# Output weights of a fused attention and token-mixing kernel: one load and cast per block, with the swapped arrangement copied on chip

## The chip, the cores and the metric

The kernel runs on one core of one Trainium2 chip. The metric is the device time of one execution in microseconds (us), the median of several runs. The engines of the core are named as in the profile: PE is TensorE (PEld its weight loads), DVE is VectorE, ACT is ScalarE, POOL is GpSimd, SP is SyncE, which here only issues transfers. Each engine works through its own instructions in order; what one engine makes and another reads is guarded by a semaphore.

## What is computed

A sigmoid attention, whose output, with the heads laid side by side, is the input of a token mixer with an output projection:

```python
# q, k, v: (8, 12, 448, 64)
scores = scale * np.matmul(q, k.transpose(0, 1, 3, 2)) - np.log(S)
attn = 1.0 / (1.0 + np.exp(-scores))
x = np.matmul(attn, v)                       # then transposed to (8, 448, 768)
wq = x @ w_q                                 # (8, 448, 64)
wk = x @ w_k
W_tok = (1.0 / np.sqrt(64)) * np.einsum('bsd,btd->bst', wq, wk)
mixed = np.einsum('bst,btd->bsd', W_tok, x)
out = np.maximum(mixed, 0.0) @ w_out         # w_out: (768, 768)
```

Inputs and output are float32; the kernel computes its matmuls in bf16.

## The kernel before

The 12 heads of each of the 8 batch entries are taken four at a time: 24 quads (a "quad" is one batch entry u and one group j of four heads). For each quad the kernel loads q, k and v (448 KB each, line 180), casts them to bf16 on GpSimd (L199), transposes q and k on TensorE (L221 for whole 128 x 128 blocks, L213 for 64 x 64 blocks) and evacuates them from PSUM to a `qk` tile on VectorE (L246 or L251). Seven score steps S(n, 0..6) of quad n follow (`scores`, L263: four matmuls, then one sigmoid on ScalarE, L268, of 128 x 896 elements), and seven value steps P(n, 0..6) (`values`, L281), which accumulate in PSUM; after the seventh VectorE evacuates the result to `xt` (L290).

When the three quads of a batch entry are done, the mixer's steps run: W (`mlp_wqk`, L345, evacuated by VectorE at L350; GpSimd then copies half of it to the other partitions at L354), x (transposes back to tokens, L304 or L321, evacuated at L309 or L334), N, U, M (the mixing, with the relu at L387) and O, the output projection. The projection is done in two ways. Batch entries 0, 1, 6 and 7 go through `out_chunk` (L481), whose matmuls contract over 128 partitions and read slots 0 to 5 of the weight tile. Entries 2 to 5 go through `out_pair` (L446), whose matmuls contract over 64 partitions, the two halves of the partitions working side by side; half y of the partitions needs block b of 64 weight rows, and as both halves need all twelve blocks, the weight tile holds each block twice, once in either half. `slot(half, b)` says where.

The weight tile `wout16` is 128 partitions x 12 slots x 768, in bf16. Slots 0 to 5 hold rows 128c to 128c + 127 of `w_out`. Slots 6 to 11 hold the same rows shifted by 64, so that each block also stands in the other half. Each slot is one load of 384 KB (`load_wout`, L527 to L535; the last slot takes two loads of 192 KB) and one cast on GpSimd (L603).

Nothing is left to a scheduler. The order of the work is written out: `PLAN` is a string with one letter for each step (S, P, W, x, N, U, M, O, and q/k transposes as a/b or q/k), worked through from left to right, and every step emits its instructions on all engines that it uses at that point. `ORDER` is the order of the loads and casts; `w0` is the pair of mixer weights, `w1` to `w12` the slots of `wout16`. Two pumps run along with the plan. `pump_loads` issues the next load on SP as long as the fifth load before it has had its cast emitted (`ld` has five buffers). `pump` emits the next cast on GpSimd as soon as its load has been issued and, for q and k, the cast two before it has been transposed, for v, the cast three before it has been used up. `pump` is called after each transposing step and after the last value step of a quad, so a cast may be emitted long before its data have landed: it then waits on GpSimd.

PSUM is one tile of eight banks, used as four pairs. `bank2` hands out the pair at the front of the list `free2`, and `release` puts it at its end at the point where the evacuation is emitted. A step that is handed a pair waits for the evacuation of what was in it.

The step that the prediction speaks of first is S(3,1), the second score step of quad 3, the row of L263 at 27.35 us; the pair that it is handed is the one in which the q and k of quad 5 were transposed. P(5,0), at 47.29 us, is handed the pair of quad 9. The lines that order the loads and casts of the weights are

```python
if nm == "w":
    if n:
        nc.gpsimd.tensor_copy(out=wout16[:, n - 1, :], in_=w32[n - 1])
```

Of the kernel before, what the change touches and what calls it, by code (L numbers as in the profile page):

```python
# [16 lines left out]
def kernel(  # L17
# [14 lines left out]
    nc = tc.nc  # L32
# [4 lines left out]
    P = 128  # L37
# [3 lines left out]
    NC = D // P  # L41
    NB = D // 2
    HALF = (slice(0, 64), slice(64, 128))
# [50 lines left out]
    wout16 = singles.tile([P, 2 * NC, D], BF16, name="wout16")  # L94
# [93 lines left out]
    def cast1(n, nm, eng):  # L188
        if twice(nm, n):
            t16 = p_c16.tile([P, 2, NI, 32, 2], BF16, tag=nm + "16", name=nm + "16")  # L190
            eng.tensor_copy(
                out=t16.rearrange("p h i d y -> p h y i d"),
                in_=ld.pop((nm, n)).rearrange("p h (y i d) -> p h y i d", y=2, d=HD)[..., 0:32],
            )
            ld[nm + "16", n] = t16
            return
        p = p_v16 if nm == "v" else p_c16
        t16 = p.tile([P, NI, 2, HD], BF16, tag=nm + "16", name=nm + "16")
        eng.tensor_copy(  # L199
            out=t16.rearrange("p i b d -> p b i d"),  # L200
            in_=ld.pop((nm, n)).rearrange("p b (i d) -> p b i d", i=NI),
        )
        ld[nm + "16", n] = t16
# [223 lines left out]

    def slot(half, b):

        if b % 2 == half:  # L430
            return b // 2
        return 6 + (b - 1) // 2 if b else 11

    def out_pair(act):

# [7 lines left out]
        for b in range(3 * part, 3 * part + 3):  # L443
            for y, (u, i) in enumerate(blocks):
                for x in range(2):
                    nc.tensor.matmul(  # L446
                        ps[HALF[x], y, 0:NB], mx[HALF[y], u, b, 64 * (i - 3 * y) : 64 * (i - 3 * y) + 64],
                        wout16[HALF[y], slot(y, b), x * NB : (x + 1) * NB],
                        start=(b == 0), stop=(b == 11),
                    )  # L450
# [66 lines left out]
    w32 = {}  # L517
# [8 lines left out]

    def load_wout(c):  # L527
        w32[c] = p_ld.tile([P, 2 * NI * HD], F32, tag="ld", name="w32")[:, 0:D]
        if c < NC:
            nc.sync.dma_start(out=w32[c], in_=moe_w_out[c * P : (c + 1) * P, :])  # L530
        elif c < 11:
            nc.sync.dma_start(out=w32[c], in_=moe_w_out[(c - 6) * P + 64 : (c - 5) * P + 64, :])
        else:
            nc.sync.dma_start(out=w32[c][HALF[0]], in_=moe_w_out[704:768, :])
            nc.sync.dma_start(out=w32[c][HALF[1]], in_=moe_w_out[0:64, :])  # L535

    IA, IB = slice(0, 4), slice(4, 7)
    KA, KB = slice(0, 3), slice(3, 7)
# [6 lines left out]
    def cols(r):  # L545
        return slice(r.start * HD, r.stop * HD)
# [9 lines left out]
        out=ident, in_=ident, compare_op=ALU.not_equal, fill=1.0, base=0,  # L556
# [8 lines left out]
    for t in wqks:  # L565
# [3 lines left out]
    ORDER = (  # L569
        "q1 k1 v0 q2 k2 k3 q3 k4 q4 v1 q5 k5 v2 w0 k6 q6 "  # L570
        "v3 q7 w1 w2 q8 k7 v4 v5 k8 q9 k9 q10 k10 w3 q11 w4 "
        "v6 w5 w6 k11 q12 k12 w7 v7 v8 q13 k13 k14 q14 q15 v9 q16 "
        "v10 k15 k16 w8 q17 q18 w9 w10 v11 k17 v12 v13 v14 q19 k18 w11 "
        "q20 w12 v15 k19 k20 k21 v16 q21 v17 k22 v18 v19 v20 q22 q23 k23 "
        "v21 v22 v23 "
    )
    ORDER = [(t[0], int(t[1:])) for t in ORDER.split()]
# [4 lines left out]
    def pump_loads():  # L582
        while len(loaded) < len(ORDER):
            nm, n = ORDER[len(loaded)]
            r, back = (ring2, 1) if twice(nm, n) else (ring, 5)
            mine = [z for z in r if z[0] == nm] if r is ring2 else r
            if len(mine) >= back and mine[-back] not in cast:
                break
            r.append((nm, n))
            if nm == "w":  # L590
                load_wout(n - 1) if n else load_weights()
            else:
                load1(n, nm, nc.sync)
            loaded.add((nm, n))

    def pump():
        while len(cast) < len(ORDER) + 2:
            nm, n = ORDER[len(cast) - 2]
            if (nm, n) not in loaded:
                break  # L600
            if nm == "w":
                if n:
                    nc.gpsimd.tensor_copy(out=wout16[:, n - 1, :], in_=w32[n - 1])  # L603
                else:
                    for h in range(2):
                        for g in range(2):
                            nc.gpsimd.tensor_copy(
                                out=wqk16[HALF[g], h::2],
                                in_=w32["qk"].rearrange("p (c n) -> p c n", c=NC)[HALF[h], g::2],
                            )  # L610
            else:
                back = 3 if nm == "v" else 2
                if n >= back and (nm, n - back) not in used:
                    break
                cast1(n, nm, nc.gpsimd)
            cast.add((nm, n))
            pump_loads()
# [5 lines left out]
    for t16, t32, r, e in ((q016, q0, IA, "v"), (q016, q0, IB, "s"), (k016, k0, KA, "g"), (k016, k0, KB, "g")):  # L623
        COPY[e](
            out=t16[:, r].rearrange("p i b d -> p b i d"),
            in_=t32[:, :, cols(r)].rearrange("p b (i d) -> p b i d", d=HD),
# [14 lines left out]
    tr_part("k", k016, KA, "v")  # L641
    used |= {("q", 0), ("k", 0)}
    pump()

    done = dict.fromkeys("SPqkKxWNUMO", 0)
# [3 lines left out]
    for t in PLAN:  # L649
# [4 lines left out]
        c = done[kind]  # L654
# [4 lines left out]
        elif t == "P":  # L659
            n, i = divmod(c, NI)  # L660
            values(n, i, tail)
            if i == NI - 1:
                used.add(("v", n))
                pump()
        elif kind in "qk":
            tr(c, kind, t)
            used.add((kind, c))
            pump()
        elif t == "K":
            tr_part("k", k016, KB, "v")  # L670
        elif kind == "x":
            tr_x(c, tail, t == "X")
        elif kind == "W":
            mlp_wqk(*divmod(c, NC), tail)
        elif kind == "N":
            mlp_wkn(c)
        elif kind == "U":
            mlp_tmp(c, t == "u")
        elif kind == "M":
            u, x = divmod(c, NC // 2)  # L680
            mlp_mix(u, x, t == "m", tail)
            if x == NC // 2 - 1:
                if u // 2 in TW:
                    chunks.extend((u // 2, ((u % 2, i), (u % 2, 6 - i))) for i in range(3))
                    if u % 2:
                        chunks.append((u // 2, ((0, 3), (1, 3))))
                else:
                    ms = range(3, NI) if u % 2 else range(3)
                    chunks.extend((u // 2, m, nb) for m in ms for nb in range(2))
        elif kind == "O":  # L690
            if (opened or chunks)[0][0] in TW:
                out_pair(t == "o")
            else:
                out_chunk(t == "o", tail)
# [29 lines left out]
```

## Time and profile before

| | |
|---|---|
| time, median of 3 runs | 204.12 us (203.43 to 205.49) |
| span of the profiled execution | 200.3 us |
| that execution's own time | not given beside the profile |
| granted TensorE clock, mean | 0.998 |
| traffic | HBM read 38.14 MB, written 11.01 MB |

| group | count | busy us | mean ns |
|---|---|---|---|
| L268 sigmoid, ACT | 168 | 157.0 | 1012 |
| L263 scores, PE | 672 | 62.4 | 360 |
| L281 values, PE | 672 | 45.9 | 350 |
| L446 projection by halves, PE | 672 | 36.3 | 323 |
| L199 casts of q, k, v, POOL | 70 | 65.2 | 930 |
| L603 casts of the weights, POOL | 12 | 9.9 | 827 |
| L246 and L251 evacuation of q and k, DVE | 23 | 25.1 | 1090 |

The span runs from the first to the last instruction. Matmuls are pipelined, so the busy time of PE and the mean of one matmul are not its pace. An engine's idle time is put down to what ended it. The twelve weight casts start between 32.6 and 102.5 us. A load of one of their blocks takes 4.8 us (median) from its issue on SP until it has landed.

### The profile page before, as it was taken

Reading aid. Unit: us, or ns where it says so; the run is one execution under the profiler, and the core shown is the slowest. Engines: PE = TensorE matmul, PEld = TensorE weight load, DVE = VectorE, ACT = ScalarE, POOL = GpSimd, SP = SyncE. Lnnn points to the kernel's source line nnn. Section 1 sums busy time; section 2 is a strip of 40 time slices with the busy share of each in tenths; the row PEclk is TensorE's granted clock in tenths of the full one; section 3 lists DMA queues with packets and bytes.
Section 4 is the critical chain, followed back from the end, with each engine's and each line's share of the span. In section 5 each row is a group of like instructions: output and inputs, shape, how many; then the busy total and the mean of one; then the engine's idle time right before and its main releaser. Section 6 shows DMA issues by size and latency. Waiting matters only on the chain.

```text
span 200.3 us, 8999 instructions
## 1 busy us (share of the span) xinstructions
PE 187.9 (94%) x3948; PEld 122.1 (61%) x3950; DVE 125.0 (62%) x165; ACT 170.3 (85%) x194; POOL 82.1 (41%) x101
## 2 busy tenths in 40 slices
PE   8995998898999999999999999999999999999990
PEld 7452564455455655665557667778678869665560
DVE  3234375667755877846786856667787774774520
ACT  4798899798989999999889799999899989975520
POOL 2467777677677647558136320305061110000000
PEclk9999999999999999999999999999999999999999
DMA  5999999999999999899999983388704443332575
GB/s 174 317 351 374 292 361 324 357 358 322 356 352 348 367 389 315 293 320 339 285 318 352 338 301 104 86 242 208 256 17 99 105 109 81 84 79 49 142 211 154
DMA packets 29799, 49.73 MB, mean 248 GB/s; under 512 B 3904, under 2 KB 26560, under 8 KB 29760
## 3 DMA queue, kind: packets, MB, share of 16 engines
q1 hardware_dynamic: 29040, 47.78, 74.2%
q10 hardware_dynamic: 720, 1.38, 1.9%
q8 instruction: 31, 0.51, 1.0%
q14 instruction: 8, 0.07, 0.1%
HBM read 38.14 MB, written 11.01 MB: 245 GB/s over the span
## 4 chain that ended last, share of the span: by engine, by line
PE 61%; DMA 26%; POOL 5%; ACT 2%; issue 1%; SPq 1%; ACTq 1%; DVE 1%; POOLq 0%; DVEq 0%
PE banks L446 14%; PE banks L263 12%; PE banks L281 11%; PE banks L481 8%; DMA k<-in_k_dram 8%; DMA q<-in_q_dram 8%; DMA v<-in_v_dram 6%; DMA out_dram<-o 5%; PE banks L345 4%; POOL q L199 2%; PE banks L376 2%; PE banks L221 2%; PE banks L321 2%; PE banks L213 2%; ACT at L268 2%
## 5 line engine op out<-in xcount | busy, mean ns | idle before, releaser
L268 ACT ACTIVATE at<-banks,bias_t 128x896 bf16<-128x896 f32 x168 | 157.0, 1012 | 11.8 <-PE banks L263 9.5
L263 PE MATMUL banks<-qk 64*64 64x448 bf16 x672 | 62.4, 360 | 1.2 <-ACT at L268 0.5
L281 PE MATMUL banks<-at,v 64*64 64x448 bf16 x672 | 45.9, 350 | 0.5 <-issue 0.5
L263 PEld LDWEIGHTS <-qk 64*64 64x64 bf16 x672 | 24.9, 105 | 21.2 <-issue 13.7
L446 PE MATMUL banks<-wout,mx 64*64 64x384 bf16 x672 | 36.3, 323 | 0.0
L199 POOL CAST v<-v 128x896 bf16<-128x896 f32 x24 | 22.4, 933 | 30.5 <-PE banks L281 21.1
L290 DVE CAST xt<-banks 128x896 bf16<-128x896 f32 x23 | 25.1, 1090 | 12.6 <-PE banks L281 12.6
L481 PE MATMUL banks<-wout,mx 128*128 128x384 bf16 (+1 forms) x174 | 31.1, 321 | 0.0
L199 POOL CAST k<-k 128x896 bf16<-128x896 f32 x23 | 21.4, 932 | 18.2 <-PE banks L213 10.5
L281 PEld LDWEIGHTS <-v 64*64 64x64 bf16 x672 | 23.1, 106 | 6.6 <-issue 0.3
L387 DVE TENSOR_SCALAR mx<-banks 128x1024 bf16<-128x1024 f32 (+2 forms) x22 | 22.7, 1044 | 6.9 <-PE banks L411 3.5
L199 POOL CAST q<-q 128x896 bf16<-128x896 f32 x23 | 21.4, 932 | 9.3 <-DMA q<-in_q_dram 5.6
L446 PEld LDWEIGHTS <-mx 64*64 64x64 bf16 x672 | 22.6, 107 | 4.0
L481 PEld LDWEIGHTS <-mx 128*128 128x128 bf16 x174 | 15.6, 98 | 12.4 <-issue 3.8
L251 DVE COPY qk<-banks 128x1792 bf16<-128x1792 bf16 x12 | 13.1, 1090 | 8.7 <-PE banks L213 7.2
L511 DVE COPY o<-banks 128x384 f32<-128x384 f32 x18 | 10.0, 556 | 9.1 <-PE banks L481 8.6
L246 DVE COPY qk<-banks 128x1792 bf16<-128x1792 bf16 x11 | 12.0, 1091 | 5.5 <-PE banks L221 5.3
L455 DVE COPY o<-banks 128x768 f32<-128x768 f32 x14 | 13.4, 955 | 2.4 <-PE banks L446 2.3
L334 DVE COPY xn<-banks 128x1024 bf16<-128x1024 bf16 (+1 forms) x15 | 9.7, 654 | 5.3 <-PE banks L321 5.2
L345 PE MATMUL banks<-xt,wqk 128*128 128x448 bf16 x48 | 12.6, 354 | 0.3 <-DVE o L511 0.3
L603 POOL CAST wout<-w 128x768 bf16<-128x768 f32 x12 | 9.9, 827 | 5.8 <-DMA w<-in_moe_w_out_dram 5.6
L511 ACT COPY o<-banks 128x384 f32<-128x384 f32 x9 | 4.4, 484 | 7.7 <-PE banks L481 6.9
(60 smaller groups left out, 158.5 us busy)
## 6 DMA issues: line engine op xcount, KB each, us to landing
q<-in_q_dram SPq DMA_DIRECT2D x24, 448.0 KB, 5.8
v<-in_v_dram SPq DMA_DIRECT2D x24, 448.0 KB, 5.3
k<-in_k_dram SPq DMA_DIRECT2D x23, 448.0 KB, 6.0
out_dram<-o SPq DMA_DIRECT2D x48, 192.0 KB, 3.2
w<-in_moe_w_out_dram SPq DMA_DIRECT2D x11, 384.0 KB, 4.8
out_dram<-o ACTq DMA_DIRECT2D x6, 192.0 KB, 3.2
w<-in_moe_w_out_dram SPq DMA_DIRECT2D x2, 192.0 KB, 6.0
k<-in_k_dram SPq DMA_DIRECT2D x1, 256.0 KB, 5.2
```

The lines of the kernel that those rows point to most:

```text
L199: eng.tensor_copy(out=t16.rearrange("p i b d -> p b i d"), in_=ld.pop((nm, n)).rearrange("p b (i d) -> p b i d", i=NI),)
L251: nc.vector.tensor_copy(out=qk[n].rearrange("p t h i n -> p t h (i n)"), in_=ps[:, :, 0 : 2 * S].rearrange("p h (t x) -> p t h x", t=2),)
L263: nc.tensor.matmul(sc[HALF[h], g, 0:S], qk[n][HALF[g], 1, h, i, :], qk[n][HALF[g], 0, h].rearrange("p i n -> p (i n)"), start=True, stop=True,
L268: nc.scalar.activation(at, sc[:, :, 0:S], ACTF.Sigmoid, bias=bias_t, scale=attn_scale)
L281: nc.tensor.matmul(ps[HALF[g], h, 0:S], ld["v16", n][HALF[h], i, g, :], ats[n, i][HALF[h], g, :], start=(i == 0), stop=(i == NI - 1),)
L290: nc.vector.tensor_copy(out=xt(u, j)[:, :, 0:S], in_=ps[:, :, 0:S])
L345: nc.tensor.matmul(ps, wqk16[:, c, :], xt(u, c // 2)[:, c % 2, 0:S], start=(c == 0), stop=(c == NC - 1),)
L387: nc.vector.tensor_scalar(dst, ps, moe_scale, 0.0, ALU.mult, ALU.max)
L446: nc.tensor.matmul(ps[HALF[x], y, 0:NB], mx[HALF[y], u, b, 64 * (i - 3 * y) : 64 * (i - 3 * y) + 64], wout16[HALF[y], slot(y, b), x * NB : ...
L455: COPY["s" if act else "v"](out=o, in_=ps[:, :, 0:NB])
L481: nc.tensor.matmul(ps, mxs[w][:, 2 * S * c + m * P : 2 * S * c + (m + 1) * P], wout16[:, c, w0:w1], start=(c == 0), stop=(c == NC - 1),)
L511: COPY["s" if act else "v"](out=o[:, nb * NB : (nb + 1) * NB], in_=ps)
```

## The change

`w7` to `w12`, the six shifted loads with their casts, are gone. After the cast of slot c on GpSimd, VectorE copies the lower half of slot c to the upper half of slot 6 + c, and the upper half to the lower half. Each block again stands in both halves, in another slot than before for the second copies, so `slot` changes. The two copies are emitted in `pump`, right where the cast is emitted, so they stand in VectorE's order at the place that VectorE's instructions had reached at that moment. In the built program four of them (for w1 and w2) come between the xt evacuation of quad 1 and the qk evacuation of quad 5, and eight (for w3 to w6) between the qk evacuations of quads 8 and 9. The first copy of each pair waits for a semaphore of GpSimd.

```diff
     def slot(half, b):
-        if b % 2 == half:
-            return b // 2
-        return 6 + (b - 1) // 2 if b else 11
+        return b // 2 + (0 if b % 2 == half else NC)
...
     def load_wout(c):
         w32[c] = p_ld.tile([P, 2 * NI * HD], F32, tag="ld", name="w32")[:, 0:D]
-        if c < NC:
-            nc.sync.dma_start(out=w32[c], in_=moe_w_out[c * P : (c + 1) * P, :])
-        elif c < 11:
-            nc.sync.dma_start(out=w32[c], in_=moe_w_out[(c - 6) * P + 64 : (c - 5) * P + 64, :])
-        else:
-            nc.sync.dma_start(out=w32[c][HALF[0]], in_=moe_w_out[704:768, :])
-            nc.sync.dma_start(out=w32[c][HALF[1]], in_=moe_w_out[0:64, :])
+        nc.sync.dma_start(out=w32[c], in_=moe_w_out[c * P : (c + 1) * P, :])
...
     ORDER = (
         "q1 k1 v0 q2 k2 k3 q3 k4 q4 v1 q5 k5 v2 w0 k6 q6 "
         "v3 q7 w1 w2 q8 k7 v4 v5 k8 q9 k9 q10 k10 w3 q11 w4 "
-        "v6 w5 w6 k11 q12 k12 w7 v7 v8 q13 k13 k14 q14 q15 v9 q16 "
-        "v10 k15 k16 w8 q17 q18 w9 w10 v11 k17 v12 v13 v14 q19 k18 w11 "
-        "q20 w12 v15 k19 k20 k21 v16 q21 v17 k22 v18 v19 v20 q22 q23 k23 "
+        "v6 w5 w6 k11 q12 k12 v7 v8 q13 k13 k14 q14 q15 v9 q16 "
+        "v10 k15 k16 q17 q18 v11 k17 v12 v13 v14 q19 k18 "
+        "q20 v15 k19 k20 k21 v16 q21 v17 k22 v18 v19 v20 q22 q23 k23 "
         "v21 v22 v23 "
     )
...
                 if n:
                     nc.gpsimd.tensor_copy(out=wout16[:, n - 1, :], in_=w32[n - 1])
+                    for h in range(2):
+                        nc.vector.tensor_copy(
+                            out=wout16[HALF[1 - h], NC + n - 1, :], in_=wout16[HALF[h], n - 1, :]
+                        )
```

## The prediction

> **What bounds the kernel now.** I read the page first (shares of the engines, the slices), then the timelines of VectorE, GpSimd and TensorE around the weight casts, then the waits, and last the granted clock at the end of the span.
>
> ```profile
> span 200.3 us, 8999 instructions
> PE 187.9 (94%) x3948; PEld 122.1 (61%) x3950; DVE 125.0 (62%) x165; ACT 170.3 (85%) x194; POOL 82.1 (41%) x101
> ...
> DMA  5999999999999999899999983388704443332575
> ```
>
> Each digit of the last line is a slice of 5 us. The transfers are full until 115 us and half empty after, but TensorE is busy 54.15 of the 55 us from 60 to 115, and 39.99 of the next 40. So from 60 us on TensorE sets the pace, ScalarE (51.38 of 55) close behind. Transfers count before 60 us, where TensorE has short waits for casts.
>
> VectorE's timeline (start, length, then the idle time before it):
>
> ```profile
> 24.86 1.09 DVE L290 CAST xt<-banks 128x896 bf16<-128x896 f32 x1 [1.38 <-PE banks L281]
> 25.99 1.09 DVE L246 COPY qk<-banks 128x1792 bf16<-128x1792 bf16 x1
> ...
> 43.52 1.09 DVE L246 COPY qk<-banks 128x1792 bf16<-128x1792 bf16 x1 [0.37 <-PE banks L221]
> 45.08 1.09 DVE L246 COPY qk<-banks 128x1792 bf16<-128x1792 bf16 x1 [0.46 <-PE banks L221]
> ```
>
> GpSimd's timeline around the first six weight casts:
>
> ```profile
> 32.56 1.80 POOL L603 CAST wout<-w 128x768 bf16<-128x768 f32 x2 [0.52 <-DMA w<-in_moe_w_out_dram]
> 34.42 0.56 POOL L354 COPY wq<-wqk 64x448 bf16<-64x448 bf16 x1
> ...
> 46.49 0.83 POOL L603 CAST wout<-w 128x768 bf16<-128x768 f32 x1
> ...
> 48.71 0.83 POOL L603 CAST wout<-w 128x768 bf16<-128x768 f32 x1
> ...
> 50.88 0.83 POOL L603 CAST wout<-w 128x768 bf16<-128x768 f32 x1
> 52.02 0.83 POOL L603 CAST wout<-w 128x768 bf16<-128x768 f32 x1 [0.32 <-DMA w<-in_moe_w_out_dram]
> ```
>
> In the changed order four copies (w1, w2) stand on VectorE between the first two rows of its fence, and eight (w3 to w6) between the last two. Each engine works in order. A pair of copies waits for its cast, and the casts end at 33.39, 34.36, and, for w3 to w6, from 47.32 to 52.85: up to 8 us after VectorE gets there. That is the whole case.
>
> **The change part by part.**
>
> *Removed.* Seven transfers on SP (six blocks of 384 KB) and six casts of 827 ns on GpSimd (5.0 us), all from 51.75 us on. At the 335 GB/s of 55 to 115 us, 2.36 MB are 7.0 us of transfers. Worth: TensorE idles 1.2 us in that stretch, ScalarE waits some 3 us from 60 to 120, mostly for matmuls. I take nothing, and keep -3 as the other end.
>
> *Added.* Twelve copies of 64 x 768 bf16 within SBUF on VectorE. No row shows this form. SBUF-sourced casts took 227 ns (128 elements) and 426 ns (512): 0.16 + 0.00052 us an element, so 0.56 for 768; the lower end is the fixed 0.16. I take 0.56, the PSUM-sourced bf16 copies being no quicker (690 ns for 1024). By themselves, 12 x 0.56 = 6.7 us beside 75 us of VectorE idle time would be cheap. [...]
>
> *First stall.* VectorE is free at 24.86 + 1.09 = 25.95 and waits until 33.39. Two copies to 34.51, two more to 35.63, then the qk evacuation of quad 5 (1.09) to 36.72. Its bank pair is the one that the score step S(3,1) takes: the plan rotates four pairs, and between them only S(2,6), S(3,0) and part of P(2) go ahead. S(3,1) is the 27.35 row of L263:
>
> ```profile
> 27.35 0.36 PE L263 MATMUL banks<-qk 64*64 64x448 bf16 x4
> ```
>
> TensorE stops there and resumes at 36.72: 9.4 us late. ScalarE has two sigmoids in hand (S(3,1)'s was the fifth of those from 24.71, 0.906 each: 28.33); with 0.5 us from score to sigmoid it gets S(3,1) at 37.2, **8.9 us late**. With copies of 0.16 it is 8.0.
> Queued behind: xt, two xn, and L350, which GpSimd's L354 reads. L354 goes from 34.42 to about 41, so GpSimd, with nine casts behind it, stops 7 us as well, and the loads after five more (each load waits for the cast five before it). The q8 load, k7, v4, v5 and k8 are in by then, so the wait for k7's cast (0.92 us at 37.05) is covered, with ScalarE's two gaps after it: **-1.05**.
>
> *Second stall.* Let T be the end of quad 8's k transposes (43.35 before, about 51.2 now). VectorE evacuates them and reaches w3's copies at T + 1.25. GpSimd needs T for k10's cast (two cast buffers): T + 1.5; w3's cast T + 2.4, which frees the buffer that w6 is loaded into. From issue to the end of the cast a w block took 47.34 to 52.85 = 5.5 us in full queues (median landing 4.8, shortest 4.5); the queue has just drained, so I take 4.0 + 0.83 and 0.1: w6 is cast at T + 7.2, its and the last of w5's copies to T + 8.3, quad 9's evacuation to T + 9.4. P(5,0) takes that bank pair; it stood at 47.29 = T + 3.94. So **+5.5**. Ends: 0, if the casts of w3 to w6 are through when VectorE gets there; 8, with the landing as before and longer copies.
> Quad 11's wait for its k cast (0.66 at 55.29) is covered by then: **-0.7**.
>
> *The clock.* The page shows full clock until the tail:
>
> ```profile
> 199.00:199.50 0.50, 0.00 (x0) 1.00 0.00 0
> 199.50:200.30 0.80, 0.00 (x0) 0.62 0.00 0
> ```
>
> (window, TensorE busy, granted clock, transfers). The last matmul ended at 195.61, and 0.62 over 0.8 us is half clock from about 199.7: 4.1 us after. The start shows the way back: the 32 zero matmuls took 3.59 us, 106 ns each, and quad 0's k transposes at 5.2 are the first at full pace, 4.1 us after the first matmul. Stall one leaves TensorE idle 9 us, stall two 6. Each time I count 4.1 us at half clock. From 27.35 to 31.45 TensorE did about 3.2 us of matmuls by their full-clock pace (0.19 per 448 columns, 57 ns per transpose); half clock does 2.05, so 1.5 us is lost: **+2.9** for both. Ends: 0, and 4.1 if TensorE had no slack at all. [...]
>
> Sum: 8.9 - 1.05 + 5.5 - 0.7 + 2.9 = **+15.6 us**. After 60 us nothing gives it back: TensorE's order is fixed and it has 0.85 us of idle time from 60 to 115. The profile shows a span of 200.3, not that execution's own time; the runs' median 204.12 is 3.8 above it, which I leave as it is: 215.9 of span, **219.7 us**.
>
> **Rivals.**
>
> *Only the first stall.* TensorE being 8 us late, GpSimd has w3 to w6 cast before VectorE needs them. For: the transfers run on until the ring of five is full. Against: L354 holds GpSimd too, and k10's cast stands before w3's. Then 8.9 - 1.05 - 0.7 + 1.5 = 8.6: 212.8. Chance 0.13.
>
> *The relief outweighs the stalls.* The saved 7.0 us of transfers bring the casts of 55 to 115 us forward, where the chain of waits runs through a v load, stores and a q cast at 82 to 98 us. It decides if VectorE's wait costs under 3 us, that is if w1 were cast by about 28 or TensorE had a free pair to go on with. Against: w1 lands at 32.5, behind loads that the change leaves alone. It gives -3: 201. Chance 0.05, one fifth of it within 1%.
>
> *A clock that stays low.* If the thin work after a stall doesn't raise the clock, half clock lasts from 37 to 61: another 7 us or more, 227. For: TensorE's matmuls fill only three quarters there. Against: at half clock they fill it. Chance 0.08.
>
> That the change does something else than it says is out: the built order has the twelve copies, each pair with its wait for GpSimd, and the transfers are gone.
>
> **How the numbers follow.** My case has 0.74. Its own range is 213 (shorter copies, no clock loss) to 223.5 (8 for the second stall, the rest as summed less rounding). The range reaches down to the second case with short copies, 211, and leaves out the relief and the low clock, 0.13 together. One per cent, 2 us, is what the runs' spread (203.43 to 205.49) can tell from nothing. Slower by more: 0.74 + 0.13 + 0.08 = 0.95; faster 0.04; within 0.01.
>
> **What would show it.** On VectorE a wait for GpSimd's wout cast of some 7.4 us ahead of the copies at 26, and waits of about 5 us in sum in the second group; L263 with an idle time of 9 us at about 27.7, L281 one of some 6 us near 56; L354 of GpSimd near 41 with a wait for L350; a granted clock under 1 after each; copies of 0.56. I am wrong if the second group's waits are short, if TensorE passes S(3,1) with quad 5 still in its bank, or if the lag at 60 us shrinks before the end.

## The result and the profile after

| | before | changed |
|---|---|---|
| median of the runs shown together | 204.12 us (203.43 to 205.49) | 221.30 us (221.26 to 223.31) |
| span of the profiled execution | 200.3 us | 219.4 us |

The changed kernel is slower: ratio 1.0869, 95% interval 1.0771 to 1.0968. (The ratios here and below compare undisturbed runs alone, so that they can differ by up to one per cent from the quotient of the medians.) The changed kernel's profiled execution took 221.3 us, 1.9 above its span, and in every run that has both numbers the two differ by 1.7 to 2.0. So the profile of before, with its span of 200.3, is of an execution of about 202.2, a quick one. Between the two profiles 19.1 us have to be accounted for, between the medians 17.2.

The page of the changed kernel (busy time of each engine, then slices of 5.5 us):

```profile
span 219.4 us, 8994 instructions
...
PE 191.7 (87%) x3950; PEld 123.6 (56%) x3950; DVE 131.7 (60%) x177; ACT 170.5 (78%) x194; POOL 76.8 (35%) x95
...
PE   8987922999309999999999999899999999999991
...
PEclk9999985799967999999999999999999999999999
```

TensorE's matmul time is nearly what it was (191.7 for 187.9); its idle time went from 12.4 to 27.7 us. Most of it lies in two holes, the slices with 2 and 2 and with 3 and 0, and the granted clock falls in or right after each. VectorE's timeline of the changed kernel shows what stands at those places (start, length, operation, idle time before it and what ended it):

```profile
25.48 1.09 DVE L290 CAST xt<-banks 128x896 bf16<-128x896 f32 x1 [1.39 <-PE banks L281]
34.25 1.98 DVE L597 COPY wout<-wout 64x768 bf16<-64x768 bf16 x4 [7.68 <-POOL wout L595]
36.15 1.08 DVE L246 COPY qk<-banks 128x1792 bf16<-128x1792 bf16 x1
...
53.72 1.09 DVE L246 COPY qk<-banks 128x1792 bf16<-128x1792 bf16 x1 [0.37 <-PE banks L221]
56.28 0.72 DVE L597 COPY wout<-wout 64x768 bf16<-64x768 bf16 x2 [1.46 <-POOL wout L595]
59.45 1.45 DVE L597 COPY wout<-wout 64x768 bf16<-64x768 bf16 x2 [2.45 <-POOL wout L595]
61.63 2.62 DVE L597 COPY wout<-wout 64x768 bf16<-64x768 bf16 x4 [0.73 <-POOL wout L595]
```

L597 is the new copy, L595 the weight cast. VectorE waits 7.68 us for w1's cast with quad 5's evacuation behind it, and between 54.8 and 64.25 it does nothing but copies and waits for them. TensorE, in the same kernel:

```profile
37.28 0.59 PE L263 MATMUL banks<-qk 64*64 64x448 bf16 x4 [8.68 <-DVE qk L246]
...
65.30 0.96 PE L281 MATMUL banks<-at,v 64*64 64x448 bf16 x8 [8.55 <-DVE qk L246]
```

The first is S(3,1), the second P(5,0): each waits for the evacuation that stands behind the copies, for the bank pair that it is handed. In the trace of before neither step waited.

### The profile page after: what moved, and what is told of

The parts are those of the page before. It is cut to its first block, busy times and chain, and to the rows that moved or that the text cites. A ratio compares the mean times of both kernels' runs of the same rounds, so it can differ in the third digit from the quotient of the medians.

```text
span 219.4 us, 8994 instructions
## 1 busy us (share of the span) xinstructions
PE 191.7 (87%) x3950; PEld 123.6 (56%) x3950; DVE 131.7 (60%) x177; ACT 170.5 (78%) x194; POOL 76.8 (35%) x95
## 4 chain that ended last, share of the span: by engine, by line
PE 67%; DMA 16%; ACT 4%; DVE 4%; POOL 3%; issue 2%; SPq 1%; ACTq 1%; POOLq 0%; DVEq 0%
PE banks L263 14%; PE banks L444 13%; PE banks L281 12%; PE banks L479 11%; DMA k<-in_k_dram 6%; PE banks L345 5%; ACT at L268 4%; DMA v<-in_v_dram 3%; DMA q<-in_q_dram 3%; PE banks L376 2%; DMA w<-in_moe_w_out_dram 2%; PE banks L213 2%; DMA out_dram<-o 2%; PE banks L321 2%; DVE wout L597 2%
## 5 line engine op out<-in xcount | busy, mean ns | idle before, releaser
L263 PE MATMUL banks<-qk 64*64 64x448 bf16 x672 | 64.2, 364 | 9.7 <-DVE qk L246 8.7
L281 PE MATMUL banks<-at,v 64*64 64x448 bf16 x672 | 47.3, 359 | 8.9 <-DVE qk L246 8.6
L444 PE MATMUL banks<-wout,mx 64*64 64x384 bf16 x672 | 37.2, 323 | 1.0 <-issue 1.0
L281 PEld LDWEIGHTS <-v 64*64 64x64 bf16 x672 | 23.8, 109 | 16.0 <-issue 9.1
L387 DVE TENSOR_SCALAR mx<-banks 128x1024 bf16<-128x1024 f32 (+2 forms) x22 | 22.7, 1044 | 7.8 <-PE banks L411 4.3
L444 PEld LDWEIGHTS <-mx 64*64 64x64 bf16 x672 | 23.1, 107 | 5.5 <-issue 1.8
L479 PEld LDWEIGHTS <-mx 128*128 128x128 bf16 x174 | 15.5, 98 | 12.4 <-issue 3.7
L354 POOL COPY wq<-wqk 64x448 bf16<-64x448 bf16 x7 | 3.9, 556 | 32.0 <-DVE wqk L350 32.0
L597 DVE COPY wout<-wout 64x768 bf16<-64x768 bf16 x12 | 6.7, 555 | 12.4 <-POOL wout L595 12.3
```

The costliest lines, as they stand in the source:

```text
L263: nc.tensor.matmul(sc[HALF[h], g, 0:S], qk[n][HALF[g], 1, h, i, :], qk[n][HALF[g], 0, h].rearrange("p i n -> p (i n)"), start=True, stop=True,
L281: nc.tensor.matmul(ps[HALF[g], h, 0:S], ld["v16", n][HALF[h], i, g, :], ats[n, i][HALF[h], g, :], start=(i == 0), stop=(i == NI - 1),)
L387: nc.vector.tensor_scalar(dst, ps, moe_scale, 0.0, ALU.mult, ALU.max)
L444: nc.tensor.matmul(ps[HALF[x], y, 0:NB], mx[HALF[y], u, b, 64 * (i - 3 * y) : 64 * (i - 3 * y) + 64], wout16[HALF[y], slot(y, b), x * NB : ...
L479: nc.tensor.matmul(ps, mxs[w][:, 2 * S * c + m * P : 2 * S * c + (m + 1) * P], wout16[:, c, w0:w1], start=(c == 0), stop=(c == NC - 1),)
```

## The experiments

"W" is the theory that the time goes into VectorE's in-order wait, "C" that the copies themselves cost it, "D" that the missing transfers are worth much. All ratios are to the kernel before on the same chip, with 95% intervals.

**late: the copies where the casts are long done**

`swap(n, h)` is the copy of one half; the list `waiting` holds the copies that are still to be emitted.

```diff
-                    for h in range(2):
-                        nc.vector.tensor_copy(
...
+                    if n in (1, 2, 3, 4, 5, 6):
+                        waiting.extend((n, h) for h in range(2))
...
             scores(*divmod(c, NI))
+            if waiting and c >= 54 and (c - 54) % 2 == 0:
+                swap(*waiting.pop(0))
```

> The twelve copies of the change, but emitted one at a time after every second score step from S(7,5) to S(10,6), some 55 to 85 us, when all six casts are long done. Theory W (the time went into VectorE's in-order wait for casts that come late): no VectorE wait for GpSimd's weight casts, no TensorE wait over 1.5 us, clock full throughout, 201 to 205 us, so within 1% of the kernel before or up to 3 us better by the missing transfers. Theory C (the copies themselves, lengthened by sharing with GpSimd, cost the time): 6.7 us of copies stay on VectorE, 208 us or more.

Measured: 204.68 us against 204.76, ratio 1.0031 (0.9991 to 1.0072). The copies in this kernel (shortest, median and longest in ns, then first and last start in us):

```profile
L574 DVE COPY wout<-wout x12: 353/356/1055, 61.2 to 85.9; 64x768 bf16<-64x768 bf16 x12
```

No VectorE wait for a weight cast is left; the longest TensorE wait is 1.4 us, for a k cast. The same twelve copies, moved by some 25 us, cost nothing that can be told from none, and neither do the six loads and casts that are saved bring anything. The expected range was met, but not the full clock: in the profile, which is of the longest of the twelve runs (206.56 us), it fell twice for 3.4 us (mean 0.57 from 18 to 22 us, 0.61 from 38 to 42).

**nocopy: the transfers' worth alone**

```diff
-        return b // 2 + (0 if b % 2 == half else NC)
+        return b // 2
...
-                    for h in range(2):
-                        nc.vector.tensor_copy(
...
```

> The change without its copies: second copies of the weights are left out and both halves read slots 0 to 5, so the output of batch entries 2 to 5 is not the reference's. It measures what the six missing loads and casts are worth alone. Theory W: 201 to 204.5, since TensorE had 1.2 us of idle time where the transfers were. Rival D (transfers bounded the stage from 55 to 115 us): 197 to 201.

Measured: 203.79 us against 204.76, ratio 0.9997 (0.9938 to 1.0056). Six loads of 384 KB and six casts fewer, without any copy, make no difference that can be told from none. D falls.

**tiny: the waits with copies of two elements**

`slot` is the one of nocopy.

```diff
-                            out=wout16[HALF[1 - h], NC + n - 1, :], in_=wout16[HALF[h], n - 1, :]
+                            out=wout16[HALF[1 - h], NC + n - 1, 0:2], in_=wout16[HALF[h], n - 1, 0:2]
```

> The twelve copies in their place, but of 2 elements of each partition in place of 768 (the rest of the second copies is left out, both halves read slots 0 to 5). Theory W: the waits stay, so 217 to 220, only the 2 to 3 us of copies that end a stall are gone; two TensorE waits of 7 to 8 us. Theory C: without the copy time 204 to 206.

Measured, in two runs of 220.60 and 221.25 us: 220.92 us against 204.76, ratio 1.0859 (1.0759 to 1.0958); the changed kernel's was 1.0869. TensorE's two waits are still 8.7 and 7.0 us. So C falls: nearly the whole loss is there with copies that move next to nothing. The expectation of 2 to 3 us less was too much. The copies lie in part inside the wait for the next cast; and though the evacuation that ends TensorE's second wait starts 1.6 us earlier (62.54 for 64.17), by 70 us only 0.7 us of the lead is left (69.59 for 70.33 at L387); the mean clock of the profiled execution was 0.953, that of the changed kernel's 0.959. The lengths of the copies, in tiny and then in the changed kernel:

```profile
L597 DVE COPY wout<-wout x12: 165/166/767, 34.6 to 62.2; 64x2 bf16<-64x2 bf16 x12
```

```profile
L597 DVE COPY wout<-wout x12: 352/354/1083, 34.2 to 63.3; 64x768 bf16<-64x768 bf16 x12
```

A copy of two elements took up to 767 ns here, with a median of 166. The longest copy of the changed kernel, 1083 ns, started at 59.8 and ended at 60.90, with a v cast on GpSimd beside it from 59.76 to 60.69.

**pool: the copies on GpSimd**

```diff
-                        nc.vector.tensor_copy(
+                        nc.gpsimd.tensor_copy(
```

> The twelve copies in their place, issued by GpSimd right after each cast. Theory W: nothing waits on VectorE, GpSimd gets 12 x 0.6 to 0.9 us and loses six casts, 203 to 206. Rival: GpSimd's casts of q and k behind the copies come later and with them the loads (each waits for the cast five before it), TensorE waits 1 to 3 us more at 35 to 60 us, 206 to 208.

Measured: 211.82 us against 204.76, ratio 1.0410 (1.0334 to 1.0486): half of the loss, and more than the rival's 206 to 208. (The shortest of its six runs took 210.01, the longest of the kernel before beside it 207.01.) A copy takes 822 ns there, and the casts of q and k queue behind them. TensorE's row of quad 7's k transposes, in this kernel:

```profile
40.07 0.93 PE L221 MATMUL banks<-ident,k 128*128 128x128 bf16 x7 [2.76 <-POOL k L199]
```

The wait was 0.92 us before; 2.3 us for a weight cast and 1.9 us for quad 11's k come on top, and these seven matmuls run at half clock (0.50 from 40 to 42 us; 0.93 us for what took 0.56).

**first_stall and second_stall: one group of copies in place, the other late**

```diff
+                    if n in (3, 4, 5, 6):
+                        waiting.extend((n, h) for h in range(2))
+                    else:
+                        for h in range(2):
+                            swap(n, h)
```

This is first_stall, with the rest as in late; second_stall has (1, 2) in the condition.

> Copies of w1 and w2 in their place, those of w3 to w6 emitted one at a time after score steps from S(7,5) on. Theory W: only the first wait is left, VectorE waits about 7.7 us at 26, TensorE about 8.7; with 1.4 for the clock and 1 us won back the lag is 9 to 10: 213 to 215. The rival that only one of the waits decides the change's loss would give either 219 to 222 or 204 to 206 here.

> Copies of w3 to w6 in their place, those of w1 and w2 later. Theory W: VectorE gets to w3's copies at 44.6, w6 is cast at 52.9, two to four copies and one evacuation behind that TensorE goes on at 55.5 in place of 47.3: 8.2, with the clock and what is won back 8 to 9.5, so 212 to 214. If the two losses add up, this and the first-stall kernel exceed the kernel before by 17 us together; if the second is only as long as the first made it, this one is under 208.

Measured: 214.38 us, ratio 1.0440 (1.0384 to 1.0495), and 213.41 us, ratio 1.0378 (1.0322 to 1.0433), both against 205.35. One TensorE wait of 8.3 us is left in the first, one of 8.1 us in the second. The losses are 9.0 and 8.1 us; together 17.1, and the whole change loses 17.2. They add up.

**before_copies: the change without its savings.** The copies are put into the kernel before; w7 to w12 are kept.

```diff
+                    for h in range(2) if n <= NC else ():
+                        nc.vector.tensor_copy(
+                            out=spare[HALF[1 - h], n - 1, :], in_=wout16[HALF[h], n - 1, :]
+                        )
```

> The kernel before, with all its twelve loads and casts, and the change's twelve copies in their place into a spare tile that nothing reads. Theory W: the missing transfers were worth nothing, so the time is the changed kernel's, 219.5 to 223. Rival D (the transfers' relief pays back part of the stalls): 224 or more.

Measured: 221.37 us (218.08 to 221.80) against 205.35, ratio 1.0692 (1.0585 to 1.0798). With all the transfers kept the median is that of the changed kernel (221.37 for 221.30), and no run took the 224 of rival D: the savings pay nothing back that these runs could show.

**warm: TensorE kept busy through the stalls**

```diff
     for t in PLAN:
+        if t == "S" and done["S"] == 22:
+            fill(36)
+        if t == "P" and done["P"] == 35:
+            fill(36)
```

> The changed kernel with 36 zero matmuls of 512 columns (7.8 us) ahead of S(3,1) and again ahead of P(5,0), into a bank pair that is free. If the half clock after the stalls costs 1.4 and about 1 us as the two traces read, the clock stays full and the time is 218 to 219.5. If the clock costs nothing, because VectorE and ScalarE pace the work after a stall, 221 to 222.

Measured: 219.63 us against 205.35, ratio 1.0666 (1.0600 to 1.0733), with a mean clock of 0.999. That is 1.7 below before_copies, which ran beside it, but the intervals overlap; the total does not settle it. The trace does, for the stretches behind the stalls. In this kernel S(3,1), S(4,4) and P(5,0) stand at

```profile
37.41 0.38 PE L263 MATMUL banks<-qk 64*64 64x448 bf16 x4 [0.91 <-DVE qk L246]
...
46.28 0.38 PE L263 MATMUL banks<-qk 64*64 64x448 bf16 x4
...
64.46 0.76 PE L281 MATMUL banks<-at,v 64*64 64x448 bf16 x12 [0.38 <-DVE qk L246]
```

From S(3,1) to S(4,4) the changed kernel needs 10.46 us (37.28 to 47.74), this one 8.87 (37.41 to 46.28); from P(5,0) to the first evacuation of an output chunk 8.18 us (65.30 to 73.48), and here 6.91 (64.46 to 71.37). The clock costs 1.6 and 1.3 us. In the profiled run the lead was lost again by 134 us, in two waits of TensorE (0.92 and 0.66) for which the profile names no cause; what they are is open.

**late_fill and before_fill: more fillers in the thin start**

```diff
-        "SSPPaPSbSSFqkSFFSFa",
+        "SSPPaPSbSSFFFFFFqkSFFSFa",
...
-        "SqPkSSPaSbSUSXSPPPM",
+        "SqPkSSPaSFFbSUSXSPPPM",
```

> The late copies, and seven more zero matmuls of 512 columns in two places where TensorE waits for a cast: five ahead of quad 3's transposes (1.39 us of waiting at 16.3 in the trace of before) and two ahead of quad 7's k transposes (0.92 at 36.1). The profile of the late kernel had half clock for 3.4 us at about 19 and again at 39. If these dips cost time as they did after the stalls (1.3 to 1.6 each), 201.5 to 203.5, and faster than the kernel before by up to 1.5%. If the work there is paced by the casts anyway, 204 to 205.5, no difference.

> The kernel before with the same seven zero matmuls, as the control: what the fill alone does. If it works in the late kernel, then here as well, 201.5 to 203.5; any difference between the two is the worth of the copies on chip, expected within 1%.

Measured: 206.05 us, ratio 1.0010 (0.9965 to 1.0055), and 205.47 us, ratio 1.0027 (0.9983 to 1.0071), against 205.02. The clock stayed full at both places in the two profiles (1.00 from 14 to 24 and from 34 to 44 us), as it had in the kernel before, and nothing was won. That fits a stretch paced by the casts (in late_fill TensorE still waits 1.4 us for a k cast), but no run shows that pace by itself. No version was found that beats the kernel before; late equals it with 2.36 MB less to load.

## Why the prediction was right, and where it was off

**The mechanism** held in each step: the place of the copies in VectorE's order, the wait for GpSimd, the evacuation behind it, the bank pair, TensorE stopping at S(3,1) and at P(5,0). Late, tiny, and the two single stalls show it: with the waits and next to no copying the loss is there, with the copies and no waits it is not.

**First stall.** TensorE was forecast 9.4 us late at S(3,1); the traces have 37.28 for 27.35, 9.9 us, of which 0.6 were there at the evacuation ahead of the copies (25.48 for 24.86). At ScalarE, where the sum has 8.9, the sigmoid of S(3,1) started 9.6 us late (37.92 for 28.29). L354, forecast to about 41 with GpSimd stopped behind it, started at 43.45, as L350 ahead of it carried the whole lag of 11.3 us (42.68 for 31.36):

```profile
43.45 0.56 POOL L354 COPY wq<-wqk 64x448 bf16<-64x448 bf16 x1 [8.16 <-DVE wqk L350]
```

The clock's part was forecast at 1.5: the lag grows from 9.9 at S(3,1) to 11.3 at S(3,4) (41.58 for 30.26). The recovery was forecast at 1.05: at S(4,4) the lag is 10.2 (47.74 for 37.54), 1.1 less. So the stall, the clock and the recovery came out as forecast; L354 was 2.4 us later.

**Second stall: the step that was mis-sized.** "the queue has just drained, so I take 4.0 + 0.83 and 0.1": forecast +5.5, measured +7.8 (P(5,0) at 65.30 for 47.29 is a lag of 18.0, after 10.2 at S(5,3)). GpSimd in the changed kernel:

```profile
55.41 0.83 POOL L595 CAST wout<-w 128x768 bf16<-128x768 f32 x1
57.71 0.93 POOL L199 CAST q<-q 128x896 bf16<-128x896 f32 x1 [1.47 <-DMA q<-in_q_dram]
58.59 0.83 POOL L595 CAST wout<-w 128x768 bf16<-128x768 f32 x1
59.76 0.93 POOL L199 CAST v<-v 128x896 bf16<-128x896 f32 x1 [0.34 <-DMA v<-in_v_dram]
60.77 1.90 POOL L595 CAST wout<-w 128x768 bf16<-128x768 f32 x2
```

The loads of w5 and w6, on SP:

```profile
55.42 1.19 SPq L527 DMA_DIRECT2D w<-in_moe_w_out_dram  x2
```

The transfer queue had been empty from 42 to 46 (shares of 0.00 and 0.05), but GpSimd's five casts came in one go behind L354, so five loads were issued from 45.96 to 49.47 and the queue was full again at once (1.05 from 48 to 50). Quad 11's q, issued at 50.53, was cast at 57.71; the w6 block, whose load was issued behind w5's, at 56.3, landed 5.4 us later, where the forecast took 4.0, and came through its cast at 62.67, where 60.8 was forecast on this kernel's T of 53.55. The upper end of the term, 8, had been worked out with the landing of full queues; that was the right row. The longer copies named for it too were an estimate of the author's, which no row of before shows; in the changed kernel four copies that began while a cast ran took 880 to 1083 ns, and from w6's cast to the evacuation it was 1.5 us in place of 1.1.

**Copies.** 0.56 us was forecast and 0.555 is the mean, by luck: a free copy took 0.35 us and one begun during a cast up to 1.08. Eight of the twelve took 352 to 355 ns, the other four 880 to 1083.

**Clock.** 2.9 was forecast for both stalls, from 4.1 us of half clock after each; the warm kernel's trace has 1.6 and 1.3, and half clock lasted 3.7 us into the work after the first stall and 3.0 after the second. The granted clock of the changed kernel (window, TensorE busy and instructions, clock, transfers' share, GB/s):

```profile
30.00:32.00 2.00, 0.00 (x0) 0.69 0.83 249
36.00:38.00 2.00, 0.72 (x8) 0.50 1.01 353
40.00:42.00 2.00, 2.00 (x48) 0.75 0.20 73
42.00:44.00 2.00, 1.97 (x37) 1.00 0.00 0
62.00:64.00 2.00, 0.00 (x0) 0.50 1.04 389
...
66.00:70.00 4.00, 4.00 (x54) 0.71 1.02 364
70.00:75.00 5.00, 5.00 (x122) 1.00 0.61 215
```

**Nothing is given back later.** The lag is 18.1 at the qk evacuation of quad 12 (74.33 for 56.23) and 19.1 at the end. In between it dips: at the sigmoids it is 18.3 up to 98 us of the trace of before, 17.2 at 116 and 19.1 from 148 on. Two TensorE waits of the trace of before are not there any more (0.3 us at 98.4, 0.5 at 114.6), and two others, 1.0 us in sum (L444), come in; the profile names no cause for them. The dip is not the work of the savings: before_copies, with all its transfers, has it too (18.6 to 17.7). Nocopy says why the saved transfers do not help: without any stall they are worth nothing.

**The rivals.** That only the first stall counts falls with second_stall; that the relief outweighs falls with nocopy; that the clock stays low falls with the rows above (1.00 again by 42 and by 70). The forecast of 219.7 was 1.6 below the median. In spans it was 3.5 short (215.9 for 219.4): 2.3 of the second stall, 0.6 from ahead of the copies, the rest from the late waits. That it came out nearer in the medians is luck: I added 3.8 from span to time, where 1.9 was right.

**The ends of the range.** Two of them do not follow from the terms named for them. With 8 for the second stall and the rest as summed the loss is 18.05 and the time 222.2; 223.5 takes the upper end of the clock's term, 4.1, as well. With copies of 0.16 us and nothing for the clock the terms are 8.0 - 1.05 + 4.7 - 0.7, which gives 215, not 213.

## What to carry to other kernels

Ask of every instruction that is moved to an in-order engine where in that engine's order it lands and when its input is ready, not how long it takes: here copies of two elements cost nearly as much as the whole ones (220.92 us for 221.30), and the whole ones cost nothing that could be told 25 us later (204.68 for 204.76). Here a saving on the busiest resource of a stage (transfers, at 98% from 55 to 115 us) was worth nothing that could be told (nocopy, ratio 0.9997), as TensorE set the pace there, and GpSimd, busy 41% of the span before, was no free place, as the casts that feed the matmuls queue on it (pool, ratio 1.0410). A queue that was refilled in one go landed a load as late as a full one: w6 took 5.4 us after the refill, and the median of the weight blocks in the kernel before was 4.8.

## What the runs showed of the hardware

- By the clock record of the changed kernel's trace the clock fell at 30.74 us, rose at 40.98, fell at 61.46 and rose at 68.29; the distances are three, six and two times 3.41. So the first fall came 2.1 us after the last matmul (28.61), the second 4.7 us after it (56.75), and the tail of before had 4.1. The first and the third of these steps ended in a fall, the second did not (same columns as above):

```profile
27.33:30.74 3.41, 1.27 (x28) 1.00 0.99 339
54.63:58.05 3.42, 2.12 (x33) 1.00 1.01 368
58.05:61.46 3.41, 0.00 (x0) 1.00 0.91 317
```

The first of these steps was not idle: it has 1.27 us of matmuls in it.

- Counted in such steps from the first record of the full clock (5.14 us in the trace of before, 6.85 in that of the changed kernel), the clock fell four times in the two traces, each time at the end of a step: at 199.70 in the first, at 30.74, 61.46 and 218.48 in the second. These four steps have 0.00, 1.27, 0.00 and 0.00 us of matmuls; the other 110 steps at full clock have 1.89 us or more, and none of them ended in a fall. The clock also fell without a long stop: in the late kernel it was 0.57 from 18 to 22 us and 0.61 from 38 to 42, where TensorE had not waited for more than 1.4 us at a time but was busy for only 0.93 us from 16 to 18 and 1.00 from 38 to 40. In the kernel before it was busy for 0.61 us from 16 to 18 and for 1.08 from 36 to 38, and the clock was 1.00 there and in the next 4 us.
- GpSimd's 64 x 768 bf16 copy within SBUF took 822 ns (pool), VectorE's 353 (the shortest in late). The four VectorE copies that began while a GpSimd cast ran in the changed kernel took 880 to 1083 ns and ended 0.2 us after that cast; the two weight casts among these took 946 and 957 in place of 827.
